# First attention round of a sigmoid-attention and gated-MLP kernel: last keys' scores ahead of last keys' values, a weight step behind x's parts, low parts reversed, one split in portions

## The chip, the cores and the metric

The kernel runs on one core of one Trainium2 chip. The metric is device time in microseconds (us); lower is better. An engine in the text is TensorE (PE in the profile, its weight loads PEld), VectorE (DVE), ScalarE (ACT), GpSimd (POOL) or SyncE (SP, which issues the DMAs).

## The reference

For each of 8 batches and 12 heads (448 positions, head size 64), attention with a sigmoid in place of the softmax; its output, heads side by side, is the input x of a gated MLP whose gate mixes positions:

```python
scores = q @ k.T / sqrt(64) - log(448)
x = sigmoid(scores) @ v                  # 8 x 448 x 768, heads side by side
h = relu(x @ w_in)                       # 8 x 448 x 1024
u, v = h[..., :512], h[..., 512:]
v_n = (v - mean(v)) / sqrt(var(v) + 1e-6)
v_s = w_spatial @ v_n + b_spatial        # over positions
out = (u * v_s) @ w_out                  # 8 x 448 x 768
```

## The kernel before, in words

The kernel makes four rounds of two batches each. A round is attention, then the MLP. Every large product is made of three products of parts: a number is split into a high part (rounded to fp32r) and a low part (the rest), and high x high, low x high and high x low are added (`TERMS`).

**Units.** Attention works on pairs of heads `(b, hp)`, two pairs at a time: one pass of the loop over n = 0, 2, ..., 10 in `first_attention` treats `units[n]` and `units[n + 1]`. The text calls such a pass unit n. Of the 448 keys of a pair 384 make three full tiles (t = 0, 1, 2 for the first pair, 4, 5, 6 for the second) and 64 remain. The remaining 64 of both pairs share one tile, t = 3 (`NFULL`): the short scores, or last keys. They use q and k unsplit, read from the loaded tile `raw`; the full tiles use the split tile `qks`.

**Steps of a unit.** Scores of a tile go to a PSUM tile `psc` (line 269 for full tiles, 257 for the short one), ACT makes the sigmoid `at` of it (line 277), and `at` is multiplied with the values into `pav` (line 307), which sums over all seven tiles. When the last of them, that of the short tile, is in, `attention_sums` splits the result into x's high and low parts: ACT casts one half (line 319), DVE the other (line 320), and DVE subtracts twice for the low parts (line 322). After that the PSUM of `pav` is free.

**PSUM.** There are four PSUM tiles of two times 512 columns, named by tags in the list `latest`, oldest first. At the head of a unit `y, z, w, x = latest`: x is the tag of the unit before, in which its `pav` still stands. The short scores take y, the full tiles take z, w, y, x, z, w in this order, and `pav` takes y again. So the fourth full tile, t = 4, is the first that needs the PSUM of the preceding `pav`.

**Order.** The program's order is the written order on each engine (`in_program_order`); each engine works its stream in that order and waits by semaphores. SP has one queue of DMA issues.

**Weights.** The MLP's weights are loaded and split into parts by a generator, `weight_steps`; `load_weights(1)` takes it one step further. A step starts, where a new block of weights begins, the DMA of the block two further on, and issues up to three DVE instructions. In the first round these steps are scattered between the attention's instructions: one each behind the full tiles t = 0, 1, 4, 5, and one between the splits of q and k for the next unit.

**Splits.** `attention_splits` casts `raw` to the high part (on ACT or DVE, line 107) and subtracts on DVE for the low part (line 108), for the columns 0 to 847 (`PART`: 384 of keys, a gap of 16, 448 of queries) at once. The unit's first full tile uses the keys 256 to 383, the second the keys 0 to 127, the third 128 to 255.

Of the kernel before, what the change touches and what calls it, by code (L numbers as in the profile page):

```python
# [14 lines left out]
P = 128  # L15
# [20 lines left out]
def attn_gmlp_kernel(  # L36
# [25 lines left out]
    nc = tc.nc  # L62
# [11 lines left out]
    FULL = NFULL * P  # L74
    GAP = 16
    REST = FULL + GAP
    PART = REST + S
# [28 lines left out]
    def split(hi, lo, src, copy):  # L106
        copy(hi, src)  # L107
        nc.vector.tensor_sub(lo, src, hi.bitcast(F32))  # L108
# [85 lines left out]
    def load_weights(n):  # L194
        for _ in range(n):
            next(weights, None)
# [27 lines left out]
    def attention_splits(b, hp):  # L224
        raw = loaded[b, hp][:, HALF:]
        s = work.tile([P, 2, 2 * S], F32R, tag="split", name=f"qks_{b}_{hp}", bufs=3)
        if b == hp == 0:

            chunk, rest, query = slice(FULL - P, FULL), slice(0, FULL - P), slice(REST, PART)
            nc.vector.tensor_copy(s[:, 0, query], raw[:, query])  # L230
            for cols in (chunk, rest):
                nc.scalar.copy(s[:, 0, cols], raw[:, cols])
            for cols in (chunk, query, rest):
                nc.vector.tensor_sub(s[:, 1, cols], raw[:, cols], s[:, 0, cols].bitcast(F32))
        else:
            scalar = b == 1 or b == 0 and hp not in (1, 2)
            split(s[:, 0, :PART], s[:, 1, :PART], raw[:, :PART], nc.scalar.copy if scalar else nc.vector.tensor_copy)
        parts_of[b, hp] = s
# [6 lines left out]
    def attention_scores(b, hp, t, tag=None, slots=big, raws=None):  # L245

        psc = banks(f"psc_{b}_{hp}_{t}", tag)
        heads = [slice(j * D, (j + 1) * D) for j in range(2)]
        if t == NFULL:
            for odd in range(2):  # L250
                if raws is None:
                    raw = loaded[b, hp + odd]
                    key, query = raw[:, :HALF], raw[:, HALF + REST :]
                else:
                    key, query = raws[:, odd, :HALF], raws[:, odd, HALF:]
                for j, rows in enumerate(heads):
                    nc.tensor.matmul(  # L257
                        psc[odd * HALF : (odd + 1) * HALF, j, :S],
                        key[rows],
                        query[rows],  # L260
                        start=True,
                        stop=True,
                    )
        else:
            s = parts_of[b, hp + t // (NFULL + 1)]
            k = (t % (NFULL + 1) + NFULL - 1) % NFULL * P
            for i, (a, e) in enumerate(TERMS):
                for j, rows in enumerate(heads):
                    nc.tensor.matmul(  # L269
                        psc[:, j, :S],  # L270
                        s[rows, a, k : k + P],
                        s[rows, e, REST:PART],
                        start=i == 0,
                        stop=i == len(TERMS) - 1,
                    )
        at = slot(slots, f"at_{b}_{hp}_{t}")[:, :, :S]
        nc.scalar.activation(at, psc[:, :, :S], AF.Sigmoid, bias=bias_s, scale=QK)  # L277
        return at
# [5 lines left out]
    def attention_values(b, hp, t, at, tag=None, apart=False):  # L284

        key = b, hp, apart and t == NFULL
        if key not in pav_of:
            pav_of[key] = banks(f"pav_{b}_{hp}_{t}", tag)
            tag_of[key] = latest[-1]
        pav = pav_of[key]  # L290
        if t == NFULL and b > 1:
            latest.sort(key=lambda tag: tag == tag_of[key])
        vt = values[b, hp]
        for odd in range(2):
            if t == NFULL:
                rows = slice(odd * HALF, (odd + 1) * HALF)
            elif (t > NFULL) == odd:
                rows = slice(0, P)
            else:
                continue  # L300
            unit = key, odd
            count[unit] = count.get(unit, 0) + 1
            total = NFULL + 1 if not apart else 1 if t == NFULL else NFULL
            start, stop = count[unit] == 1, count[unit] == total
            for j in range(2):
                heads = slice(j * D, (j + 1) * D)
                nc.tensor.matmul(  # L307
                    pav[heads, odd, :S], vt[rows, t, heads], at[rows, j], start=start, stop=stop
                )
        return pav[:, :, :S]  # L310

    def x_parts(b, hp):
        x = x_s[:, :, hp : hp + 2, (b % 2) * S : (b % 2 + 1) * S]
        return x[:, 0], x[:, 1]

    def attention_sums(b, hp, pav):

        hi, lo = x_parts(b, hp)
        nc.scalar.copy(hi[:, 0], pav[:, 0])
        nc.vector.tensor_copy(hi[:, 1], pav[:, 1])  # L320
        for i in range(2):
            nc.vector.tensor_sub(lo[:, i], pav[:, i], hi[:, i].bitcast(F32))

    def product(ps, pairs, more=(), start=True, stop=True):
# [183 lines left out]
    def loads(f, n, end=end):  # L508
        if n < end:
            f(*units[n])  # L510

    def first_attention():

        shorts = {}

        def splits(n):
            loads(attention_splits, n)

        def short_scores(n, tag):
            shorts[n] = attention_scores(*units[n], NFULL, tag)  # L520
            loads(attention_loads, n + 4)

        def short_values(n):
            pav = attention_values(*units[n], NFULL, shorts.pop(n))
            attention_sums(*units[n], pav)

        splits(0)
        for n in range(0, end, 2):
            unit = units[n]
            full = []  # L530

            def scores(t, tag=None):
                if n == 0 and t in (1, NFULL + 1):
                    splits(1 if t == 1 else 2)
                full.append((*unit, t, attention_scores(*unit, t, tag)))
                if t == 0:
                    loads(attention_loads, n + 3)
                    loads(value_loads, n + 2)
                if t > NFULL if n == 0 else t not in (2, TILES - 1):
                    load_weights(1)  # L540

            def products(tag=None):
                for args in full:
                    attention_values(*args, tag)

            if n == 0:
                for t in FIRST:
                    scores(t)
                short_scores(n, None)
                for t in SECOND:  # L550
                    scores(t)
                splits(3)
                products()
                continue
            y, z, w, x = latest
            short_values(n - 2)
            short_scores(n, y)
            for t, tag in zip((*FIRST, *SECOND), (z, w, y, x, z, w)):
                scores(t, tag)
            splits(n + 2)  # L560
            load_weights(1)
            splits(n + 3)
            products(y)
        short_values(end - 2)

    def attention(m):

# [11 lines left out]
        def splits(*ns):  # L579
            for n in ns:  # L580
                attention_splits(*units[first + n])
# [107 lines left out]
    for m in range(B // 2):  # L689
        if m == 0:  # L690
            first_attention()
        else:
            for _ in running:
                pass
# [86 lines left out]
```

## Time and profile before

| | |
|---|---|
| Median of 3 runs | 670.38 us (670.1 to 670.81) |
| Profiled execution | 670.34 us, span 668.6 us |
| Busy: PE, DVE, ACT | 664.3, 331.1, 224.3 us |
| First round's attention on PE | 4.12 to 67.27 us |
| A unit of it (short scores of n = 2 to those of n = 4) | 15.58 to 25.89 us |
| Granted TensorE clock | 1.000 |

The profile has the span from the first to the last instruction; the run takes 1.7 us more. Times in views count from the span's start. In rows with tiles, out<-in gives what is written and read, x6 the number of instructions merged into the row; a bracket gives idle time before it and what ended it. A row of merged instructions goes from the start of the first to the end of the last.

### The profile page before, as it was taken

The numbers are of one execution on the slowest core, as the hardware profiler recorded it, in microseconds if no ns is written. First come the engines' busy times: TensorE is split into PE (matmuls) and PEld (weight loads), VectorE is DVE, ScalarE is ACT, GpSimd is POOL, SyncE is SP. The second block draws the span as 40 slices with busy tenths as digits, with TensorE's granted clock in tenths as the row PEclk, the third lists the DMA queues.
The fourth block names the chain that finished last, engine by engine and source line by source line (L and its number), as shares of the span: only waits on it lengthen the run. The fifth ranks groups of instructions, "written<-read, shape, count | busy, mean of one in ns | idle before, by whom it ended". The sixth has DMA issues, their size and how long they took to land.

```text
span 668.6 us, 9058 instructions
## 1 busy us (share of the span) xinstructions
PE 664.3 (99%) x3860; PEld 510.2 (76%) x3860; DVE 331.1 (50%) x500; ACT 224.3 (34%) x264; POOL 19.4 (3%) x36
## 2 busy tenths in 40 slices
PE   9999999999999999999999999999999999999997
PEld 5554889999655588999964558899985556899997
DVE  6998899831357447231145644722024554663201
ACT  6877010021567410002176731010128663101111
POOL 0000010000000002000000001100000000110000
PEclk9999999999999999999999999999999999999999
DMA  8783222331444300002153430000216410000022
GB/s 301 264 270 125 63 63 68 109 111 54 160 152 168 112 1 1 0 1 82 57 183 104 164 112 1 0 1 1 82 56 198 129 69 1 0 1 1 0 83 82
DMA packets 22184, 57.34 MB, mean 86 GB/s; under 512 B 2816, under 2 KB 9984, under 8 KB 22144
## 3 DMA queue, kind: packets, MB, share of 16 engines
q1 hardware_dynamic: 22144, 56.76, 25.0%
q8 instruction: 30, 0.49, 0.3%
q14 instruction: 10, 0.08, 0.0%
HBM read 45.74 MB, written 11.01 MB: 85 GB/s over the span
## 4 chain that ended last, share of the span: by engine, by line
PE 99%; ACT 0%; issue 0%; ACTq 0%
PE pav L307 20%; PE pv L328 17%; PE po L328 17%; PE pu L328 17%; PE psc L269 14%; PE pg L328 11%; PE psc L257 3%; PE idle L685 1%; ACT osb L479 0%; ACTq L479 0%
## 5 line engine op out<-in xcount | busy, mean ns | idle before, releaser
L277 ACT ACTIVATE at<-psc,bias_s 128x896 f32<-128x896 f32 x168 | 154.4, 1017 | 44.8 <-PE psc L269 23.5
L307 PE MATMUL pav<-at,v 128*64 128x448 f32 (+1 forms) x768 | 134.6, 545 | 0.1
L328 PE MATMUL pu<-x_s,w_u_s 128*128 128x448 f32 x576 | 117.1, 362 | 0.0
L328 PE MATMUL po<-gs,w_out_s 128*128 128x448 f32 x576 | 116.5, 362 | 0.0
L328 PE MATMUL pv<-w_v_s,x_s 128*128 128x512 f32 x504 | 115.5, 390 | 0.0
L328 PEld LDWEIGHTS po<-gs,w_out_s 128*128 128x128 f32 x576 | 108.0, 187 | 7.2
L328 PEld LDWEIGHTS pu<-x_s,w_u_s 128*128 128x128 f32 x576 | 108.0, 187 | 7.2
L328 PEld LDWEIGHTS pv<-w_v_s,x_s 128*128 128x128 f32 x504 | 94.3, 188 | 22.4 <-issue 2.8
L307 PEld LDWEIGHTS pav<-at,v 128*64 128x64 f32 (+1 forms) x768 | 45.4, 135 | 77.3 <-issue 57.6
L269 PEld LDWEIGHTS psc<-qks 64*128 64x128 f32 x864 | 78.9, 186 | 24.2 <-issue 6.3
L269 PE MATMUL psc<-qks 64*128 64x448 f32 x864 | 95.5, 371 | 0.0
L107 ACT CAST gs<-g 128x896 fp32r<-128x896 f32 x16 | 15.1, 942 | 182.0 <-DVE g L431 182.0
L328 PE MATMUL pg<-w_sp_s,vn 128*128 128x448 f32 x352 | 71.7, 362 | 0.0
L328 PEld LDWEIGHTS pg<-w_sp_s,vn 128*128 128x128 f32 x352 | 66.0, 187 | 4.6
L431 DVE SCALAR_TENSOR_TENSOR g<-pu,g 128x896 f32<-128x896 f32 x16 | 17.4, 1090 | 87.2 <-PE pu L328 87.2
L107 DVE CAST qks<-raw 128x848 fp32r<-128x848 f32 x38 | 22.7, 597 | 63.2 <-PE po L328 58.7
L348 ACT ACTIVATE rv<-pv 128x1024 f32<-128x1024 f32 (+1 forms) x16 | 14.7, 921 | 108.4 <-PE pv L328 108.4
L597 DVE COPY whole<-pav 128x896 f32<-128x896 f32 x15 | 16.4, 1092 | 69.9 <-PE pav L307 69.9
L108 DVE TENSOR_TENSOR qks<-raw,qks 128x848 fp32r<-128x848 f32 x47 | 49.0, 1042 | 3.8 <-ACT qks L107 2.5
L483 ACT COPY osb<-po 128x896 f32<-128x896 f32 x23 | 20.9, 907 | 81.6 <-PE po L328 81.6
L352 DVE BATCH_NORM_STATS2 stats<-rv 128x6 f32<-128x512 f32 x28 | 19.0, 678 | 31.5 <-ACT rv L348 31.5
L408 DVE TENSOR_TENSOR g<-pg,b_bc 128x896 f32<-128x896 f32 x16 | 17.4, 1088 | 19.2 <-PE pg L328 19.2
(48 smaller groups left out, 274.5 us busy)
## 6 DMA issues: line engine op xcount, KB each, us to landing
raw<-qk_dram SPq DMA_DIRECT2D x47, 456.0 KB, 4.1
v<-v_dram SPq DMA_DIRECT2D x23, 448.0 KB, 5.3
out_dram<-osb SPq DMA_DIRECT2D x23, 448.0 KB, 2.6
wraw<-w_in_dram SPq DMA_DIRECT2D x12, 512.0 KB, 5.4
wraw<-w_out_dram SPq DMA_DIRECT2D x6, 512.0 KB, 3.5
last<-qk_dram SPq DMA_DIRECT2D x3, 448.0 KB, 4.7
wraw<-w_sp_dram SPq DMA_DIRECT2D x4, 256.0 KB, 4.8
out_dram<-osb SPq DMA_DIRECT2D x2, 224.0 KB, 2.1
```

Of the source, the lines that this page charges most:

```text
L107: copy(hi, src)
L108: nc.vector.tensor_sub(lo, src, hi.bitcast(F32))
L257: nc.tensor.matmul(psc[odd * HALF : (odd + 1) * HALF, j, :S], key[rows], query[rows], start=True, stop=True,)
L269: nc.tensor.matmul(psc[:, j, :S], s[rows, a, k : k + P], s[rows, e, REST:PART], start=i == 0, stop=i == len(TERMS) - 1,)
L277: nc.scalar.activation(at, psc[:, :, :S], AF.Sigmoid, bias=bias_s, scale=QK)
L307: nc.tensor.matmul(pav[heads, odd, :S], vt[rows, t, heads], at[rows, j], start=start, stop=stop)
L328: nc.tensor.matmul(ps, st, mv, start=start and i == 0, stop=stop and i == len(ops) - 1)
L352: nc.vector.bn_stats(stats, rv[:, i])
L408: nc.vector.tensor_add(g, pg[:, :, :S], bb)
L431: nc.vector.scalar_tensor_tensor(g, pu[:, :, :S], 0.0, g, op0=ALU.max, op1=ALU.mult)
L483: nc.scalar.copy(osb, whole_of.pop(es)[:, :, :S])
L597: copy(whole, pav)
```

## The change

Four edits, all in the first round.

1. In units 2 to 10 the short scores of this unit are issued ahead of the last value products of the unit before (`short_values`, with x's parts in it) instead of behind them.
2. The weight step between `splits(n + 2)` and `splits(n + 3)` moves behind the next unit's `short_values`; unit 2 has none, and one is added behind the last unit's.
3. In `attention_sums` the two subtractions change places: the half that DVE casts comes first. It holds for the first round alone, since only `first_attention` calls it.
4. The split of the second pair of the first unit (`b == 0 and hp == 1`) is done in two portions, columns 256 to 847 (the keys of t = 4 and the queries) and then 0 to 255, each with a cast and a subtraction on DVE.

```diff
@@ attention_splits
+        elif b == 0 and hp == 1:
+
+            for cols in (slice(FULL - P, PART), slice(0, FULL - P)):
+                split(s[:, 0, cols], s[:, 1, cols], raw[:, cols], nc.vector.tensor_copy)
         else:
@@ attention_sums
-        for i in range(2):
+        for i in (1, 0):
             nc.vector.tensor_sub(lo[:, i], pav[:, i], hi[:, i].bitcast(F32))
@@ first_attention
             y, z, w, x = latest
+            short_scores(n, y)
             short_values(n - 2)
-            short_scores(n, y)
+            if n > 2:
+                load_weights(1)
             for t, tag in zip((*FIRST, *SECOND), (z, w, y, x, z, w)):
                 scores(t, tag)
             splits(n + 2)
-            load_weights(1)
             splits(n + 3)
             products(y)
         short_values(end - 2)
+        load_weights(1)
```

In the rows below a name ends in the unit's pair and tile and a running number: `psc_2_3` is the score tile of pair 2 and t = 3, `pav_0_0` the value sums of unit 0. The lines behind the edits are four to six higher after the change.

PE between the values of unit 0 and the fourth full tile of unit 2, before:

```order
L307 MATMUL pav_0_0_215<-at_0_6_208,v_0_85 64x448 x2
L307 MATMUL pav_0_0_215<-at_0_3_168,v_0_85 64x448 x4
L257 MATMUL psc_2_3_236<-raw_2_87 64x448 x2
L257 MATMUL psc_2_3_236<-raw_3_138 64x448 x2
L269 MATMUL psc_2_0_245<-qks_2_172 128x448 x6
L269 MATMUL psc_2_1_263<-qks_2_172 128x448 x6
L269 MATMUL psc_2_2_278<-qks_2_172 128x448 x6
L269 MATMUL psc_2_4_287<-qks_3_212 128x448 x6
```

and after:

```order
L311 MATMUL pav_0_0_217<-at_0_6_210,v_0_85 64x448 x2
L261 MATMUL psc_2_3_230<-raw_2_87 64x448 x2
L261 MATMUL psc_2_3_230<-raw_3_138 64x448 x2
L311 MATMUL pav_0_0_217<-at_0_3_170,v_0_85 64x448 x4
L273 MATMUL psc_2_0_247<-qks_2_174 128x448 x6
L273 MATMUL psc_2_1_265<-qks_2_174 128x448 x6
L273 MATMUL psc_2_2_280<-qks_2_174 128x448 x6
L273 MATMUL psc_2_4_289<-qks_3_214 128x448 x6
```

The row that completes `pav_0_0` now stands behind the short scores, directly ahead of the full tiles.

ACT at the same place (the cast of `x_s` is the copy of x's high half), before:

```order
L277 ACTIVATE at_0_6_208<-psc_0_6_201,bias_s 128x2x448
L107 CAST qks_3_212<-raw_3_138 128x848
L319 CAST x_s<-pav_0_0_215 128x448
L277 ACTIVATE at_2_3_241<-psc_2_3_236,bias_s 128x2x448
L277 ACTIVATE at_2_0_252<-psc_2_0_245,bias_s 128x2x448
```

and after:

```order
L281 ACTIVATE at_0_6_210<-psc_0_6_203,bias_s 128x2x448
L107 CAST qks_3_214<-raw_3_138 128x848
L281 ACTIVATE at_2_3_235<-psc_2_3_230,bias_s 128x2x448
L323 CAST x_s<-pav_0_0_217 128x448
L281 ACTIVATE at_2_0_254<-psc_2_0_247,bias_s 128x2x448
```

The copy of x now stands behind the sigmoid of the short scores.

DVE around x's parts of unit 2 (`w_sp_s` and `wval` belong to weight steps), before:

```order
L108 TENSOR_TENSOR qks_4_318<-raw_4_170,qks_4_318 128x848
L107 CAST w_sp_s<-wraw_258 128x512
L108 TENSOR_TENSOR w_sp_s<-wraw_258,w_sp_s 128x512
L108 TENSOR_TENSOR qks_5_325<-raw_5_254,qks_5_325 128x848
L320 CAST x_s<-pav_2_0_328 128x448
L322 TENSOR_TENSOR x_s<-pav_2_0_328,x_s 128x448 x2
L129 TENSOR_SCALAR wval_373<-wraw_272 128x512
```

and after:

```order
L108 TENSOR_TENSOR qks_4_320<-raw_4_172,qks_4_320 128x848
L108 TENSOR_TENSOR qks_5_323<-raw_5_256,qks_5_323 128x848
L324 CAST x_s<-pav_2_0_326 128x448
L326 TENSOR_TENSOR x_s<-pav_2_0_326,x_s 128x448 x2
L107 CAST w_sp_s<-wraw_260 128x512
L108 TENSOR_TENSOR w_sp_s<-wraw_260,w_sp_s 128x512
L129 TENSOR_SCALAR wval_375<-wraw_274 128x512
```

The weight step's two rows went from between the subtractions for q and k to behind x's parts.

## The prediction

> **What bounds the kernel now.** I read the page first, then the chain of work in order of time, the waits of the first round, and single instructions there.
>
> ```profile
> span 668.6 us, 9058 instructions
> PE 664.3 (99%) x3860; PEld 510.2 (76%) x3860; DVE 331.1 (50%) x500; ACT 224.3 (34%) x264; POOL 19.4 (3%) x36
> PEclk9999999999999999999999999999999999999999
> ```
>
> TensorE is busy for 99% of the span, so only time that its stream of matmuls gains or loses counts. The chain lies on PE from 0.76 us to 665 us, so its pieces are a timetable of that stream (start, length, tile, line, matmuls):
>
> ```profile
> 4.12 2.83 PE psc L269 x18
> ...
> 7.86 2.15 PE psc L269 x18
> 10.01 5.57 PE pav L307 x32
> 15.58 0.75 PE psc L257 x8
> 16.34 3.91 PE psc L269 x36
> ...
> 36.96 4.05 PE psc L269 x36
> 41.01 5.57 PE pav L307 x32
> ...
> 57.71 3.97 PE psc L269 x36
> 61.68 5.58 PE pav L307 x32
> 67.27 28.79 PE pv L328 x126
> ...
> 180.76 1.67 PE psc L257 x16
> 182.42 0.75 PE pav L307 x8
> ...
> 186.98 4.66 PE pav L307 x24
> 191.64 3.81 PE psc L269 x36
> ```
>
> Everything edited lies before 67.27. A unit there is 8 short-score matmuls (0.75), 36 full-score matmuls and 32 value matmuls (5.57). The same 36 scores take 3.81 in a later round and 3.91 to 4.05 here, so PE loses 0.1 to 0.24 us in each of five units, at most about 1 us in all. The waits between 10.01 and 67.27 say on what (total, times, longest):
>
> ```profile
> PEld psc L269 <- ACT at L277: 0.9, 5, 0.2
> PEld psc L269 <- DVE x_s L322: 0.7, 3, 0.3
> DVE x_s L320 <- ACT x_s L319: 1.0, 1, 1.0
> DVE wval L129 <- DMA wraw<-w_in_dram: 0.3, 1, 0.3
> ```
>
> Row two is the important one: a load of keys waits for the low parts of x. Those subtractions are the last readers of the value sums, and the fourth full tile of the next unit (t = 4) is written into their banks (tag x of the list z, w, y, x, z, w). In three of five units they are already late. The third row says that DVE's cast of x waits for ACT's, although the two copy different halves. Unit 2 shows the whole path:
>
> ```profile
> 15.40 0.93 PE L257 MATMUL psc<-raw 64*64 64x448 f32 x8
> 15.65 0.53 ACT L319 CAST x_s<-pav 128x448 fp32r<-128x448 f32 x1 [2.13 <-PE pav L307]
> 16.22 0.62 DVE L320 CAST x_s<-pav 128x448 fp32r<-128x448 f32 x1 [0.97 <-ACT x_s L319]
> 16.49 1.01 ACT L277 ACTIVATE at<-psc,bias_s 128x896 f32<-128x896 f32 x1 [0.30 <-PE psc L257]
> 16.49 6.40 ACT L277 ACTIVATE at<-psc,bias_s 128x896 f32<-128x896 f32 x7 [0.30 <-PE psc L257]
> 16.76 1.15 DVE L322 TENSOR_TENSOR x_s<-pav,x_s 128x448 fp32r<-128x448 f32 x2
> 17.82 0.42 DVE L107 CAST w_sp_s<-wraw 128x512 fp32r<-128x512 f32 x1
> 18.27 0.69 DVE L108 TENSOR_TENSOR w_sp_s<-wraw,w_sp_s 128x512 fp32r<-128x512 f32 x1
> ```
>
> PE's sums end at 15.58, ACT copies, DVE casts 0.04 after ACT's end at 16.18 (it had been idle for 0.97), and the banks are free at 17.91. Unit 6 shows what that wait costs:
>
> ```profile
> 36.88 1.11 PEld L269 LDWEIGHTS psc<-qks 64*128 64x128 f32 x12 [0.70 <-ACT x_s L319]
> 38.17 0.50 PEld L269 LDWEIGHTS psc<-qks 64*128 64x128 f32 x6 [0.18 <-ACT at L277]
> 38.92 0.19 PEld L269 LDWEIGHTS psc<-qks 64*128 64x128 f32 x2 [0.25 <-DVE x_s L322]
> 37.73 1.15 DVE L322 TENSOR_TENSOR x_s<-pav,x_s 128x448 fp32r<-128x448 f32 x2
> ```
>
> The subtractions end at 38.88, the load for t = 4 starts at 38.92, which is 1.96 after the phase began at 36.96, and the phase takes 4.05.
>
> **The change, part by part.**
>
> *Scores ahead of values.* PE does the same work, with the last-keys value matmuls (0.75) moved behind the short scores. The order on PE itself is free: 24 values, 8 short scores, 8 values take 4.66 + (1.67 - 0.75) + 0.75 = 6.33, where 32 values and 8 short scores took 5.57 + 0.75 = 6.32. What matters is the path of x. Two things happen to it. PE has the 0.75 of short scores no longer between the end of the sums and the full scores, so t = 4 arrives sooner after the sums. And ACT, which serves its stream in order, now has the short scores' sigmoid ahead of the copy of x.
>
> Let T be the end of the short scores. The sigmoid starts 0.16 later (15.40 + 0.93 = 16.33, then 16.49) and holds ACT for 0.90 ((6.40 - 1.01)/6). The sums are finished at T + 0.75, before ACT is free, so the copy starts at T + 1.06. Then: copy 0.53, hop 0.04, DVE's cast 0.62, hop 0.04, subtractions 1.15, hop to PE 0.04. The key load for t = 4 can start at T + 3.48. The full scores begin at T + 0.75, so the load stands 2.73 after the start of its phase, where unit 6 had 1.96. The wait sets the load's time and everything behind it follows, so the phase takes 4.05 + 0.77 = 4.82. I charge the excess one for one: behind the waiting load PE has nothing else in its stream, t = 5 and 6 and the values queue up, and they in turn delay the next unit.
>
> The 0.1 that PE lost on the short scores' sigmoid (first row of the waits) goes, since that sigmoid is early now; it is inside the 4.82, as t = 4 is placed by the later wait alone. The sigmoids behind stay ahead of PE: that of t = 2, for which the value sums wait, is ACT's third after the copy of x, so it ends near T + 1.6 + 3 x 0.9 + 0.1 = T + 4.4, and PE gets there at T + 5.6.
>
> *Low parts reversed.* Both subtractions must be done before the banks are free, so the order saves nothing. It may cost: before, the first one used ACT's half and started 0.08 before DVE's own cast had ended (16.76 against 16.84); now it needs that cast. The hop between dependent DVE instructions is 0.04 (6.39 + 0.60, then 7.03, below), so 0.12 per unit, already in the chain above. Bounds: 0 and 0.12; I take 0.12, as every dependent pair in the trace shows the hop.
>
> *Weight step behind x's parts.* Four steps move by one place and the one of unit 2 goes to the end; each is up to three DVE instructions, and its DMA two steps ahead. Ahead of x's cast DVE now has only the two subtractions of q and k, so the 0.3 of unit 6 cannot recur, but ACT's copy is later than that anyway: worth nothing more. DVE's load by window:
>
> ```profile
> 10.01:67.27 57.26, 57.24 (x413) 28.32 (x413) 50.67 (x89) 43.78 (x52) 0.00 (x0) 1.00 0.68 235
> 67.27:96.06 28.79, 28.79 (x127) 23.85 (x128) 27.00 (x56) 3.63 (x4) 3.37 (x6) 1.00 0.19 55
> ```
>
> (The third busy time is DVE.) It needs 50.67 of 57.26 us, and the window gets longer, so the steps still end before the next cast of x. The last step (0.42 + 0.69 for its cast and subtraction) falls into the 28.79 us behind, where DVE has 1.8 us free and PE waits for none of it: nothing. On SP the loads of two q/k tiles pass a weight load each; DVE waited 0.3 us for such a load once, so 0 to 0.3 per unit, and I take 0 because the weight is used two steps later. POOL's stream is untouched.
>
> *Second unit in portions.* In the start:
>
> ```profile
> 3.63 1.16 DVE L234 TENSOR_TENSOR qks<-raw,qks 128x128 fp32r<-128x128 f32 x3
> 6.39 0.60 DVE L107 CAST qks<-raw 128x848 fp32r<-128x848 f32 x1 [1.60 <-DMA raw<-qk_dram]
> 7.03 1.04 DVE L108 TENSOR_TENSOR qks<-raw,qks 128x848 fp32r<-128x848 f32 x1
> ```
>
> Low parts were complete at 8.07, when PE, at 7.86, had begun to use them. The first portion (592 of 848 columns) takes about 0.45 and 0.75 and ends near 7.67; the rest ends near 8.45, about when t = 5 wants it. The 18 scores there take 2.15, and half of 3.81 is 1.90: gain between 0 and 0.25; I take 0.15, nearer the upper end, since the first low part is 0.4 earlier. Two more DVE instructions (832 columns in three take 1.16, 848 in one 1.04) are covered by the 9.94 to 15.6 in which DVE only has weights.
>
> *Sum.* Before, from 10.01 to 67.27: 57.26. After: five times 24 values, 5 x 4.66 = 23.30; five times short scores, short values and full scores, 5 x (0.92 + 0.75 + 4.82) = 32.45; the last unit's 32 values, 5.58. Together 61.33, so +4.07, less 0.15 at the start: +3.9. The profiled execution took 670.34 us for its span of 668.6 (median of the runs 670.38), so 674.2.
>
> **Rivals.**
>
> *ACT and DVE copy x side by side.* If DVE's cast waited for the sums alone, it would start at T + 0.82, and the load at T + 0.82 + 0.62 + 0.04 + 1.15 + 0.04 = T + 2.67, 1.92 after the phase's start, as in unit 6 before. Phase 4.01, sum 23.30 + 5 x 5.68 + 5.58 = 57.28: with the start, 670.2, no change. For it: the two copies touch different halves of the tile. Against: the cast at 16.22. The Trainium skill, PSUM — Partial Sum Buffer, under "Specifications (TRN2)", states that ScalarE and VectorE can read PSUM in parallel as long as they hit different banks; by that the sum would be this rival's, but the 0.97 idle until ACT's end shows a wait that the program makes. Chance 0.09.
>
> *The banks are no limit (not slower).* If t = 4 found its banks free, as in later rounds, each phase would take 3.81: 23.30 + 5 x 5.48 + 5.58 = 56.28, so -0.98 - 0.15: 669.2. It decides from a load at or before about 1.9 after the phase's start. Against: row two of the waits, with a shorter path. Chance 0.03.
>
> *DVE gets late.* If the weight steps pile up and the subtractions of q and k push x's cast behind ACT's copy, by one step of 0.42 + 0.69 in three units, +3.3: 677.5. For it: DVE's 50.67 of 57.26. Against: units of 11.1 instead of 10.3 us. Chance 0.05.
>
> *The clock falls in the new gaps.* The cold start shows the price: 18 scores in 2.83 instead of 1.90. Five half phases at that rate add 4.7: 678.9. Against: the granted clock is 9 in all slices, through the 0.25 gaps too. The Trainium skill, TensorE: Matmul & The Clock Gate, "A second HAM failure mode: psum-queue depth-cycling", tells of a clock that oscillates from frequent short idling between groups; its "The HAM clock gate" asks for an idle window of about 3.4 us, which gaps of 0.8 are not. No run here shows which holds. Chance 0.03.
>
> **How the numbers follow.** The forecast (0.80) is 674.2. Without the reversal's hop it is 0.6 lower, 673.6; with a sigmoid holding ACT for its full 1.01 it is 0.55 higher; a weight wait of 0.3 in half of the units adds 0.7, 675.4. A one-for-one charge that is 0.2 too high in each unit takes 1.0 more off: 672.6. Range 672.6 to 675.4; the rivals outside hold 0.20. What this measurement can tell from no change is 0.2%, 1.34 us, so 669.0 to 671.7. Same: 0.09 and most of the 0.03, faster what is left of that; slower 0.88.
>
> **What would show it.** In the changed trace the waits of PE's loads for DVE's x parts should go from 0.7 us over three units to about 4 over five, the full-score pieces from 3.9-4.05 to about 4.8, DVE's cast should start at ACT's end of copy, and that copy right behind a sigmoid. The 18 scores at 7.86 should take 2.0. Score pieces of 4.0 or less would prove me wrong, through a cast that starts before ACT's copy ends; so would pieces at 3.8, through banks that t = 4 doesn't wait for.

## The result and the profile after

The changed kernel takes 677.4 us (677.07 to 677.73, 5 runs) against 670.38 us: 1.0103 times as long (95% interval 1.0091 to 1.0114). Slower was forecast, by 3.9 us; it is 7.0 us. The direction held, and so did the path over which x frees its PSUM; in four of the five units one link of that path starts on a wait that the forecast did not have.

Three of the executions behind the comparisons below, one of the kernel before and one each of two versions, took 1724 us in place of about 670, and the ratios leave them out.

The chain of work in order of time, of the changed kernel (start, length, what), through the first two units and the end of the round:

```profile
7.83 2.00 PE psc L273 x18
9.83 4.66 PE pav L311 x24
14.49 0.98 PE psc L261 x8
15.47 0.02 issue
15.50 0.02 ACTq L281
15.51 0.05 issue
15.56 1.01 ACT at L281
16.57 0.43 ACT x_s L323
17.00 0.02 issue
17.02 0.64 DVE x_s L324
17.66 0.02 issue
17.68 1.17 DVE x_s L326 x2
18.85 0.14 issue
18.98 2.08 PE psc L273 x18
21.07 4.66 PE pav L311 x24
25.73 0.91 PE psc L261 x8
26.64 0.80 PE pav L311 x8
27.43 0.02 issue
27.45 0.02 ACTq L281
27.47 0.05 issue
27.52 0.74 ACT at L281
...
30.95 2.08 PE psc L273 x18
33.02 4.66 PE pav L311 x24
...
68.90 5.57 PE pav L311 x32
74.47 28.79 PE pv L332 x126
```

Before, this chain lay on PE through the whole round. Now it goes from PE to ACT's sigmoid, ACT's copy of x, DVE's cast, DVE's two subtractions and back to PE: the path that the forecast priced. Two things are to be read. Counted from one unit's values to the next, unit 2 lasts from 9.83 to 21.07, 11.24 us; unit 4 from 21.07 to 33.02, and all four later units average (68.90 - 21.07)/4 = 11.96. And in unit 2 the sigmoid follows the short scores (L261), while in unit 4 it follows the value products behind them (L311). The waits of PE and ACT agree (total, times, longest):

```profile
PE psc L273 <- DVE x_s L326: 6.7, 5, 1.5
```

```profile
ACT at L281 <- PE pav L311: 12.4, 4, 3.2
ACT at L281 <- PE psc L261: 1.8, 1, 1.8
```

The short scores' sigmoid waits for `pav` four times, and for its own scores (L261) once. Counted in the kernel, unit 4's short scores are complete with PE's matmul number 126; the next four are the preceding unit's last-keys values, and in the chain the sigmoid starts behind those. The kernel offers a reason, which the first experiment tests: the buffer that the sigmoid writes. The sigmoids of the round go round a list of seven buffers (`big`), and a unit has seven tiles, so from unit 4 on the short tile gets the buffer of the preceding unit's short tile. That buffer is read by the very values that the change put behind the scores. Unit 2 is spared because unit 0 made its tiles in another order, t = 0 first, so unit 2's short tile gets the buffer of unit 0's t = 0.

### The profile page after: what moved, and what is told of

It reads as the page before. It is cut to its first block, busy times and chain, and to the rows that moved or that the text cites. A ratio compares the mean times of both kernels' runs of the same rounds, so it can differ in the third digit from the quotient of the medians.

```text
span 675.8 us, 9071 instructions
## 1 busy us (share of the span) xinstructions
PE 664.8 (98%) x3860; PEld 510.7 (76%) x3860; DVE 332.1 (49%) x502; ACT 224.4 (33%) x264; POOL 19.4 (3%) x36
## 4 chain that ended last, share of the span: by engine, by line
PE 97%; DVE 1%; ACT 1%; issue 0%; ACTq 0%
PE pav L311 19%; PE pv L332 17%; PE po L332 17%; PE pu L332 17%; PE psc L273 12%; PE pg L332 10%; PE psc L261 3%; DVE x_s L326 1%; ACT at L281 1%; PE idle L691 0%; DVE x_s L324 0%; ACT x_s L323 0%; ACT osb L483 0%; ACTq L281 0%; ACTq L483 0%
## 5 line engine op out<-in xcount | busy, mean ns | idle before, releaser
L311 PE MATMUL pav<-at,v 128*64 128x448 f32 (+1 forms) x768 | 134.7, 543 | 0.1
L311 PEld LDWEIGHTS pav<-at,v 128*64 128x64 f32 (+1 forms) x768 | 45.9, 136 | 75.8 <-issue 57.5
L107 DVE CAST qks<-raw 128x848 fp32r<-128x848 f32 (+2 forms) x39 | 22.8, 586 | 61.3 <-PE po L332 57.6
L108 DVE TENSOR_TENSOR qks<-raw,qks 128x848 fp32r<-128x848 f32 (+2 forms) x48 | 48.8, 1023 | 1.3
```

What stands on the lines that cost most here:

```text
L311: nc.tensor.matmul(pav[heads, odd, :S], vt[rows, t, heads], at[rows, j], start=start, stop=stop)
```

## The experiments

Theory S: the loss is x's path plus this buffer wait. Rival C: the later start of the sigmoid comes from the way PE's progress is counted. Rival W: it comes from DVE's moved weight steps. The kernel before ran on the same chip in each group of comparisons.

**Another buffer for the short scores' sigmoid** (all four edits kept):

```diff
             y, z, w, x = latest
+            if n > 2:
+                big[0], big[1] = big[1], big[0]
             short_scores(n, y)
```

> The changed kernel, with one more edit: from unit 4 on, the short scores' sigmoid is written to the buffer that the preceding unit's t = 0 had, and t = 0 takes the one of the preceding short tile. Theory S (the sigmoid waits because the buffer that it overwrites is still read by the preceding unit's last-keys values): ACT then starts it 0.16 us after the short scores as in unit 2, units 4 to 10 fall from 11.96 to 11.24 us like unit 2, and the time from 677.4 to about 674.5. Rival C (the wait comes from how PE's progress is counted when scores stand between values, not from the buffer): stays at 677.4. Rival W (DVE's moved weight steps make x late): stays at 677.4.

Measured: 674.82 us (4 runs), 1.0063 (1.0047 to 1.0078). In its chain the units start at even steps:

```profile
10.02 4.66 PE pav L311 x24
...
21.25 4.66 PE pav L311 x24
...
32.48 4.66 PE pav L311 x24
...
66.17 5.57 PE pav L311 x32
```

All units now last (66.17 - 10.02)/5 = 11.23 us, as unit 2 did. ACT at the head of unit 4, in the changed kernel and in this one:

```profile
27.52 1.01 ACT L281 ACTIVATE at<-psc,bias_s 128x896 f32<-128x896 f32 x1 [3.16 <-PE pav L311]
28.43 0.53 ACT L323 CAST x_s<-pav 128x448 fp32r<-128x448 f32 x1
```

```profile
26.98 1.01 ACT L281 ACTIVATE at<-psc,bias_s 128x896 f32<-128x896 f32 x1 [2.45 <-PE psc L261]
27.88 0.52 ACT L323 CAST x_s<-pav 128x448 fp32r<-128x448 f32 x1
```

The sigmoid is released by its scores again. A buffer alone, with every engine's order unchanged, gives 2.6 us back; C and W fall. The rest of the loss stays, as S says, and PE still waits for x's parts in each unit, for 4.1 us in all:

```profile
PE psc L273 <- DVE x_s L326: 4.1, 5, 0.8
```

**The order of scores and values undone, the other three edits kept:**

```diff
-            short_scores(n, y)
             short_values(n - 2)
             if n > 2:
                 load_weights(1)
+            short_scores(n, y)
```

> The changed kernel with the short scores put back behind the last-keys values; the other three edits stay. Theory S: all of the loss is in the order of scores and values, so no loss is left; 0.15 to 0.2 gained at the start and about 0.1 at t = 4 of units 6 and 8: about 670.1 (before 670.38). Rival W: the weight step or the reversed low parts cost by themselves, 671 or more.

Measured: 670.22 us (11 runs), 0.9993 (0.9985 to 1.0002). No loss is left in the other edits. The chain is on PE alone again, and the full scores of units 6 and 8 are not held up any more:

```profile
26.62 3.92 PE psc L273 x36
...
36.93 3.93 PE psc L273 x36
...
47.24 3.91 PE psc L273 x36
```

(Units 4, 6, 8; those of units 6 and 8 took 4.05 before.) The value products behind them take 0.06 to 0.07 longer than before, so units 6 and 8 gain 0.06 to 0.07 us each, from 10.37 and 10.38 to 10.31.

**The order alone, in the kernel before:**

```diff
-            short_values(n - 2)
             short_scores(n, y)
+            short_values(n - 2)
```

> The kernel before with the one edit that puts the short scores ahead of the last-keys values. Theory S: the whole loss, without the 0.2 gained at the start and without the reversal's 0.12 per unit: about 677.0. Rival W: most of the loss is gone, below 674.

Measured: 677.06 us (4 runs), 1.0096 (1.0082 to 1.0110). This one edit makes the whole loss.

**ACT's order undone, PE's kept.** The short scores' sigmoid is issued behind the copy of x:

```diff
             short_scores(n, y)               # scores alone
             short_values(n - 2)
+            shorts[n] = shorts[n]()          # their sigmoid
```

> The changed kernel, with PE's order kept and ACT's undone: the sigmoid of the short scores is issued behind ACT's copy of x. Theory S with x's path as the limit: the copy starts 0.07 us after the sums, so t = 4 starts 0.25 us earlier in unit 2 and 1.0 earlier in units 4 to 10, units of 11.0 us, 673.3. If instead PE loses the time in its own order (scores between values): stays near 677.

Measured: 673.72 us (4 runs), 1.0047 (1.0034 to 1.0061); units from 9.80 to 20.79 and on, 10.99 us each:

```profile
9.80 4.66 PE pav L314 x24
...
20.79 4.66 PE pav L314 x24
...
31.79 4.66 PE pav L314 x24
```

So 3.7 us of the 7.0 hang on ACT's order alone, which contains the buffer wait. In what remains two limits end together. PE's loads now wait for sigmoids, five times and 2.6 us in all, because the short scores' sigmoid, behind the copy, is late for t = 2, which reuses its PSUM tag; the scores of t = 2 end at 18.58 in unit 2 (its chain). The path of x, which the expectation reckoned with, is as late: DVE's subtractions end at 17.41 + 1.15 = 18.56, and the load for t = 4 starts 0.12 behind them.

```profile
PEld psc L273 <- ACT at L282: 2.6, 5, 0.5
```

```profile
17.41 1.15 DVE L329 TENSOR_TENSOR x_s<-pav,x_s 128x448 fp32r<-128x448 f32 x2
18.68 0.70 PEld L273 LDWEIGHTS psc<-qks 64*128 64x128 f32 x7 [0.49 <-PE psc L273]
```

This run does not separate the two.

**The fourth full tile in another PSUM tile** (on top of the buffer experiment):

```diff
-            for t, tag in zip((*FIRST, *SECOND), (z, w, y, x, z, w)):
+            for t, tag in zip((*FIRST, *SECOND), (z, w, y, z, w, x)):
```

> The kernel of the buffer experiment (short scores' sigmoid in another buffer), and the full tiles take the PSUM tags z, w, y, z, w, x in place of z, w, y, x, z, w, so that only t = 6 needs the tile of the preceding sums. If the limit is x's path through that PSUM tile: t = 4 and t = 5 then wait for sigmoids instead, 0.25 and 0.3 us, phases of 4.4 and units of 10.75, about 672.0. If that PSUM tile is not what t = 4 waits for: as the buffer experiment, about 674.5, or more by the new waits for sigmoids.

Measured: 671.54 us (10 runs), 1.0014 (1.0004 to 1.0023). Against the buffer experiment's 674.82 on another chip, and by the two ratios as well, taking x's tag out of the way of t = 4 gives 3.3 us back. A further run was made for its profile:

> The kernel of the PSUM tag experiment once more, for its profile: units of 10.75 us or a little less (671.5 was measured, 0.5 below the 672.0 expected), with PE's key loads waiting for sigmoids ahead of t = 4 and t = 5 and no wait for DVE's low parts.

It took 672.0 us; units last 10.62 us (20.85 to 31.47 and on), and the wait for DVE's low parts is gone from PE:

```profile
20.85 4.66 PE pav L311 x24
...
31.47 4.66 PE pav L311 x24
```

```profile
PEld psc L273 <- ACT at L281: 3.4, 10, 0.4
```

The ten waits for sigmoids, two per unit, are those expected at t = 4 and t = 5. The full scores of a unit take 4.29 to 4.35 us with them, against 3.91 to 4.05 in the kernel before. That these waits alone keep this version from beating the kernel before was not tried.

**The reversed low parts.** Put back in the changed kernel (`for i in range(2)`):

> The changed kernel with the low parts in the order of before. x's path is the limit of each of five units here, and the first subtraction can overlap the cast again: 0.12 us per unit, 676.8. If the order of the two does not matter: 677.4.

Measured: 677.27 us (4 runs), against 677.4; by the times that is no difference. Its chain shows one all the same:

```profile
10.03 4.66 PE pav L311 x24
...
21.13 4.66 PE pav L311 x24
...
56.61 4.66 PE pav L311 x24
```

Unit 2 lasts 11.10 us and units 4 to 8 (56.61 - 21.13)/3 = 11.83, where the changed kernel has 11.24 and 11.96: 0.13 per unit, 0.65 in five, as the forecast's 0.12 per unit. Here 0.20 of it was lost again at the start (values at 10.03 in place of 9.83). A second pair of profiles agrees: unit 2 lasts 11.10 us with the order alone, which has no reversal, and 11.23 in the buffer experiment, which has it. The times do not confirm the cost.

**The weight step and the split in portions only:**

> The kernel before with two of the edits, the weight step behind x's parts and the split in portions; order of scores and of low parts as before. If the reversal costs 0.12 us only where PE waits for x's parts: 669.9 to 670.1, the same as with the reversal or 0.1 better. Before: 670.38.

Measured: 670.02 us (11 runs), 0.9991 (0.9982 to 1.0000). It has the lowest time of the versions tried. With 1.0000 at the edge of the interval it is not shown to beat the kernel before.

## Why the prediction was wrong, point by point

- **The path of x sets the place of t = 4: right.** The chain after shows each hop of it, and each experiment that shortens it or goes round it comes within 0.5 us of the time reckoned. PE's waits for x's parts were forecast at about 4 us over five units; they are 6.7, and 4.1 once the sigmoid has another buffer.
- **Unit 2: right.** Forecast 4.66 + 0.92 + 0.75 + 4.82 = 11.15, measured 11.24. Of the 0.09, 0.07 lies in the last hop: 0.04 was taken from unit 6 before, and here PE's load starts 0.11 after the subtractions, 17.68 + 1.16 = 18.84 on DVE against 18.95. Ahead of that load, in all five units, PE's load queue has an instruction of its own that the kernel before lacks there (ns: least, median, most):

```profile
17.68 1.16 DVE L326 TENSOR_TENSOR x_s<-pav,x_s 128x448 fp32r<-128x448 f32 x2
18.95 0.22 PEld L273 LDWEIGHTS psc<-qks 64*128 64x128 f32 x2 [1.16 <-PE psc L273]
L273 PEldq EVENT_SEMAPHORE  x1: 51/51/51, 18.9 to 18.9; - x1
```

  Whether its 51 ns make most of the 0.07 was not tried. At 0.09 a unit the five are 0.4 over the forecast.
- **"The sigmoid starts 0.16 later": this step failed.** It was taken from unit 2 of the kernel before and used for all five units, with no term for a wait on the sigmoid's own buffer. In units 4 to 10 the sigmoid starts when the last-keys values are done, which makes each of them 11.96 - 11.24 = 0.72 longer, 2.9 in four. Together with the 0.4 this is the whole gap: from the first values to the gate's values 61.33 were forecast and 74.47 - 9.83 = 64.64 measured, 3.31 more. The forecast followed the PSUM tags and the engines' orders. It did not follow the buffers that the moved instruction writes. In these four units t = 2 also waits a little for that sigmoid, 0.6 us in all, a wait that the forecast had gone; it lies ahead of the longer one for x's parts. With another buffer for that sigmoid the time, 674.82, is 0.6 above the forecast's 674.2.
- **Rival "side by side": wrong.** DVE's cast starts at 17.02, right behind ACT's copy (16.46 + 0.52 = 16.98), with 1.96 idle before it. The Trainium skill, PSUM — Partial Sum Buffer, under "Specifications (TRN2)", allows ScalarE and VectorE to read different banks in parallel; no run here shows them do it, since DVE's start is put down to the end of ACT's copy in every unit. What sets that wait is not shown.
- **Rival "no limit": wrong.** PE waits for x's parts in all five units.
- **Rival "DVE gets late": wrong.** DVE waited for ACT's copy in each unit, 11.1 us in all, so it was not late. That this rival's 677.5 lies next to the measured time is chance:

```profile
DVE x_s L324 <- ACT x_s L323: 11.1, 5, 3.3
```

- **Rival "the clock falls": wrong.** The granted clock, 1.00 in this stretch with PE busy for 57.91 of the 64.64 us, does not decide it:

```profile
9.83:74.47 64.64, 57.91 (x414) 29.02 (x413) 50.37 (x87) 44.26 (x52) 0.00 (x0) 1.00 0.61 208
```

  It is 1.00 at the start of the kernel before too (4.12 to 6.95), where the same kind of matmul is much slower; so what makes the 2.83 us there, from which the forecast took this rival's price, does not show in the granted clock. What decides is how long a matmul takes (ns: least, median, most), at that start and behind the wait of unit 6 after the change:

```profile
L269 PE MATMUL psc<-qks x18: 357/572/736, 3.8 to 6.6; 64*128 64x448 f32 x18
L273 PE MATMUL psc<-qks x18: 357/360/470, 42.9 to 44.6; 64*128 64x448 f32 x18
```

  The median is 360 ns behind each of the five waits, and 359 in a later round of the kernel before.
  Of the two rules of the Trainium skill, TensorE: Matmul & The Clock Gate, the one under "The HAM clock gate" agrees: behind waits of up to 1.5 us, shorter than its idle window, the matmuls are not slower. The oscillation under "A second HAM failure mode: psum-queue depth-cycling" did not show.
- **Split in portions: forecast 0.15, measured 0.18 here (10.01 to 9.83), not shown.** The same start lay between 9.80 and 10.03 in five other profiles of kernels with the split, at 10.18 in that of the PSUM tags, and at 10.07 in the kernel with the order alone, which has no split: the spread is as large as the gain.

## What to carry to other kernels

When an instruction is moved ahead of another, list every buffer that it writes as well as those that it reads: a ring whose length equals the number of tiles per pass hands each tile the buffer of its own predecessor, and the last reader of that may be what you have just moved behind. Do it for a pass in the steady state, not for the first one, whose tiles may have been made in another order. And an exchange of order that looks free on the busiest engine is priced on the queues of its helpers: here PE's order was free, and ACT's in-order stream put a sigmoid into the path that frees PSUM.

## What the runs showed of the hardware that was not expected

PE came back from a wait of up to 1.5 us, five times within 65 us, at full speed: the 18 matmuls behind it take 360 ns each by median, as in a later round. At the start of the kernel before the median is 572 ns, and the granted clock of the profile reads 1.00 in both places: it does not show every slow matmul. A key load that must wait for DVE starts 0.11 to 0.12 us after DVE's end with the order changed, where it took 0.04 to 0.06 in the kernel before; an EVENT_SEMAPHORE instruction of 51 ns stands ahead of it in the first case alone.
